# Splitting the first layers of a fused attention + gated FFN kernel into two rounds over the batch pairs

## The chip, the cores and the metric

One core of one Trainium2 chip runs the whole kernel. The metric is the device time of one execution in microseconds (us); lower is better. Engine names below: PE is TensorE, DVE is VectorE, ACT is ScalarE, POOL is GpSimd, SP is SyncE, whose queue issues every DMA of this kernel.

## The reference

Sigmoid attention over 8 batches, 12 heads, 448 positions, head size 64, and behind it a gated feed-forward layer (3584 tokens, model size 768, hidden size 1536).

```python
scores = scale * np.matmul(q, k.transpose(0, 1, 3, 2)) - np.log(S)
attn = 1.0 / (1.0 + np.exp(-scores))
x = (attn @ v).transpose(0, 2, 1, 3).reshape(B * S, H * D)
gate = 1.0 / (1.0 + np.exp(-(x @ w_gate)))
val = x @ w_val
return (gate * val @ w_out).astype(np.float32)
```

The three weight matrices arrive as 64-bit floats; the kernel reads them as 32-bit words and turns them into 16-bit operands itself.

## The kernel before

**Attention.** A beat is one step (m, g): m runs over 24 groups of four heads of a batch, g over 7 key tiles, 168 beats in all. In a beat PE computes scores (L434, 8 matmuls of 64x64), ACT the sigmoid (L437), and PE multiplies an earlier beat's result with v (L451, 8 matmuls). Twice per m, `finish` copies one accumulator out of PSUM on ACT (L461), DVE adds the other (L468), and the sum is stored in DRAM (L473, tensors `xd`).

**Weight conversion.** A group is one 128-column-pair slice (jp, t) of the gate (t = 0) or value (t = 1) matrix, or one k of the output matrix: 12 first-layer groups for 6 d_ff tile pairs jp, and 6 output groups. A group has four chunks of 128 x 384 words. The generator `convert` runs in steps. Two steps per chunk decode the words: DVE L188, L190, L199, L200, L201, L202 and POOL L189. One further step later the chunk's largest absolute value, or its sum of absolutes, is taken (L117 on DVE beside the attention, L114 on ACT later). When the group's scale is known (for first-layer groups over a round trip through DRAM: `rowm` out, `all` back in), seven steps each make one operand: some with a POOL sum (L244), all with a 16-bit cast `whl` on POOL (L342, beside the attention) or ACT (L339, later), and in the next step the remainder on DVE (L214); one step after that the pair is sent to DRAM (L222, tensors `ad` and `oo`). `due` and `BESIDE` say how many steps are run in each tick or beat. Nine groups (`FIRST`) are converted beside the attention, three in the first visit, six output groups later.

**First layers (A visits).** The batches are handled as four pairs, by a seven-product scheme on 2 x 2 blocks (`N_OPS` = 7). A visit ("A", pr) runs 6 jp x 2 (gate, value) x 7 = 84 products; a product is 9 matmuls (L569) of 16-bit high and low parts. A product is one tick. `unit` adds the seven products up on DVE, POOL and ACT (L554, L582, L584), then come sigmoid (L730), scaling (L339), and the product of gate and value (L745 on DVE, L747 on POOL). Products fill one of 8 PSUM buffers. `load_operands` keeps a ring of 8 weight operands, up to 11 ahead with those that stay resident: 24 of the 84 stay in the `held` tiles of the hidden values (`RESIDENT`). Beside a visit the next pair's x is read from `xd` and subtracted (`load_x`, L309 on POOL, from tick 8 on every second tick) and split into the pairs of 16-bit operands `b` (`split_x`, L339 on ACT, L345 on DVE, from tick 56, `SPLIT`). Hidden values go to DRAM, those of the last pair stay (`hold`).

**Output layer (C visits).** Pairs in reversed order, 21 products of 18 matmuls each. `Operands` makes 16-bit operands `hh`, `hl` (L339, L345) from the hidden values; `OutScale` finds a scale per pair from all hidden values, over the same kind of round trip through DRAM (`rowh`, `all`). Products 0 to 5 use a scale from half of the hidden values, the later ones the whole.

The order on each engine is the order in which the program emits instructions, and an engine that waits holds up all that stands behind it:

```python
visits = [("A", pr) for pr in pairs] + [("C", pr) for pr in reversed(pairs)]
```

Of the kernel before, what the change touches and what calls it, by code (L numbers as in the profile page):

```python
# [33 lines left out]
FIRST = 9  # L34
# [10 lines left out]
SPLIT = 56  # L45
# [3 lines left out]
def sigmoid_attention_glu_kernel(ctx: ExitStack, tc: tile.TileContext, qk, v, wg, wv, wo, out):  # L49
# [154 lines left out]
    def convert(words, parts, ks, largest_of, cast):  # L204
# [5 lines left out]
        def split():  # L210

            while unsplit:
                x, sc, hl, where = unsplit.pop(0)
                nc.vector.scalar_tensor_tensor(out=hl[:, 1], in0=x, scalar=sc.s, in1=hl[:, 0], op0=ALU.mult, op1=ALU.subtract)  # L214
                unsent.append((hl, where))
# [9 lines left out]
        def high(x, sc, where):  # L225
            hl = pool.tile([P, 2, CW], F16, tag="whl", name="whl", bufs=words.held)
            cast(hl[:, 0], x, sc.s)
            unsplit.append((x, sc, hl, where))
# [65 lines left out]
    def convert_steps(n_groups, everywhere):  # L294
        return 8 * n_groups + (TAIL + 2 if everywhere else TAIL - 3)
# [10 lines left out]
    visits = [("A", pr) for pr in pairs] + [("C", pr) for pr in reversed(pairs)]  # L306
# [44 lines left out]

    def split_x(pr, cast=scaled):
# [3 lines left out]
        for at in range(len(work) + 2):  # L356
            if at >= 2:
                hi, lo = new_bs[work[at - 2]]
                n, k = work[at - 2]
                rest(lo, source(n, k), x_scales[pr].s, hi)  # L360
                if n == 2:
                    subtract(nc.gpsimd, xs[5, k], xs[2, k], xs[5, k])
            if 1 <= at <= len(work):
                n, k = work[at - 1]
                at_, half = divmod(at - 1, 2)
                if not half:
                    both = operand_pairs(at_)
# [5 lines left out]
    N_A = 2 * JPS * N_OPS  # L373
    RESIDENT = range(12, 84, 3)

    def visit_operands(v_):
        kind, _ = visits[v_]
        if kind == "A":
            return [(a_dram[jp][t][n].rearrange("p a f -> p (a f)"), [("a", jp, t, n)],
                     r if r in RESIDENT and v_ < len(pairs) - 1 else None)  # L380
                    for r, (jp, t, n) in enumerate(itertools.product(range(JPS), range(2), range(N_OPS)))]
# [4 lines left out]
    ring, resident, new_resident = [], {}, [None]  # L386

    def load_operands(most=RING + BEYOND):

        while wanted and len(ring) < most:  # L390
            source, keys, r = wanted[0]
            if r in resident:
                ring.append((resident[r], False))
            else:
                if r is None and sum(own for _, own in ring) == RING:
                    break
                a = new_resident[0]() if r is not None else xpool.tile([P, 2 * KC * P], F16, tag="A", name="A", bufs=RING)
                assert all(key in stored for key in keys), keys
                nc.sync.dma_start(out=a, in_=source)
                if r is not None:  # L400
                    resident[r] = a
# [8 lines left out]
    with tc.manual_schedule(), tc.tile_pool(name="att", bufs=2) as att, tc.tile_pool(name="sc", bufs=2, space=PSUM) as scp, \  # L410
# [47 lines left out]
        def finish(n):  # L458
# [3 lines left out]
            adds.append((x, avs.pop((n, 1))[:, :S]))  # L462
            stores.append((beat + 2, b, c, x))

        def finish_adds():
            while adds:
                x, other = adds.pop()
# [28 lines left out]
        words = Words(att, chunks(halves_of_jps[:FIRST], ()), AHEAD, 4)  # L496
        weights, n_weights, done = convert(words, halves_of_jps[:FIRST], (), max_abs, scaled_gpsimd), convert_steps(FIRST, True), 0
# [11 lines left out]
        for m in range(B * NQ):  # L509
            for g in range(7):  # L510
# [8 lines left out]
                beat += 1  # L519
                while done < n_weights and done * BESIDE < beat * n_weights:  # L520
                    next(weights)
                    done += 1
                finish_adds()
# [9 lines left out]
        beat += 2  # L533
# [101 lines left out]
    def hold(pr):  # L635
        big = {}
        for i in range(4):
            for k in range(KH):
# [3 lines left out]
                hs[pr, i, k] = big[at][:, k % 2 * S:k % 2 * S + S]  # L642

# [44 lines left out]
    def a_visit(v_):  # L688

        pr, nxt = visits[v_][1], visits[v_ + 1]  # L690
        bs.update(new_bs)
        keep = nxt == ("C", pr)
        following = next((p for kind, p in visits[v_ + 1:] if kind == "A"), None)
        x_loads = load_x(following, new_raw) if following is not None else iter(())
        splits = split_x(following) if nxt[0] == "A" else iter(())
        if keep:
            hold(pr)
            chain[0] = Operands([p for _, p in itertools.takewhile(lambda x: x[0] == "C", visits[v_ + 1:])])
# [3 lines left out]
        def tick():  # L702
# [5 lines left out]
            if p >= N_A - 22 and p % 2 == 0 and early:  # L708
# [8 lines left out]
            if p >= N_A - 6:  # L717
# [215 lines left out]
```

## Time and profile before

| | |
|---|---|
| median of 3 runs | 1271.9 us (1268.73 to 1272.67) |
| profiled execution | 1265.04 us, span 1263.3 us |
| busy, share of the span | PE 92%, DVE 70%, POOL 50%, ACT 48% |
| DMA | 244.61 MB, 68.6% of 16 engines' time |
| mean granted TensorE clock | 0.966 |

Busy time is summed for each engine, and engines overlap, so the shares do not add up. What a change in one stage is worth is read from that stage's own stretch of the span: how long it took beside the time that its matmuls need when nothing holds them. A wait is put down to the instruction that released it. The 64x64 score matmuls and the 128x128 ones have different durations, so a stretch is compared only with a stretch of the same kind.

### The profile page before, as it was taken

The page shows a single profiled execution, that of the slowest core. Times are in us where ns is not written, and L with a number is a line of the kernel's source. Part 1 is how long each engine was busy: PE and PEld are TensorE (multiplying, and loading weights), DVE is VectorE, ACT ScalarE, POOL GpSimd, SP SyncE. Part 2 cuts the span into 40 slices and gives each one's busy share as a digit, 9 for nine tenths or more (in the row PEclk, how much of TensorE's full clock was granted, in tenths as well). Part 3 has the DMA queues.
Part 4 walks back from the last instruction along what each step waited for, and adds up shares of the span by engine and source line. Part 5 has one row for each costly group of instructions (what it writes and reads, how often), then busy time and mean ns, then how long its engine had stood idle before and what let it go on. Part 6 is the DMA issues. An engine that isn't in the chain of part 4 may idle for free.

```text
span 1263.3 us, 20978 instructions
## 1 busy us (share of the span) xinstructions
PE 1161.1 (92%) x7240; PEld 564.3 (45%) x7240; DVE 889.5 (70%) x1502; ACT 610.5 (48%) x1111; POOL 632.9 (50%) x544
## 2 busy tenths in 40 slices
PE   9988777879999959999999998999994989999998
PEld 3433333334455424555445553455552445555554
DVE  5677777775378958569887897684354858676773
ACT  6754544546554356543565545544442424344240
POOL 0354656688335535356444654353255629293660
PEclk9998888889999989999999999999997999999999
DMA  8889878857699765766458864565543787776734
GB/s 295 216 229 250 243 224 234 201 169 230 198 286 201 196 137 180 230 170 178 129 184 258 188 188 117 158 162 145 139 121 78 131 269 219 241 237 209 244 114 149
DMA packets 176554, 244.61 MB, mean 194 GB/s; under 512 B 52160, under 2 KB 160960, under 8 KB 176448
## 3 DMA queue, kind: packets, MB, share of 16 engines
q1 hardware_dynamic: 176448, 243.28, 68.6%
q8 instruction: 56, 0.92, 0.3%
q14 instruction: 50, 0.41, 0.1%
HBM read 179.90 MB, written 63.32 MB: 193 GB/s over the span
## 4 chain that ended last, share of the span: by engine, by line
PE 55%; DVE 15%; DMA 10%; POOL 9%; issue 7%; ACT 3%; SPq 0%; DVEq 0%; POOLq 0%; ACTq 0%
PE un L569 49%; POOL whl L342 3%; PE sc L434 3%; PE av L451 3%; DVE whl L214 2%; POOL wf L244 2%; DVE wf L200 2%; DVE wf L199 1%; DVE wm L201 1%; DVE hl L345 1%; DMA rowh<-h02m 1%; DMA xd<-x 1%; DMA all<-rowh 1%; POOL wf L189 1%; POOL v L309 1%
## 5 line engine op out<-in xcount | busy, mean ns | idle before, releaser
L569 PEld LDWEIGHTS <-A 128*128 128x128 f16 x3888 | 382.5, 98 | 416.1 <-issue 56.7
L569 PE MATMUL un<-b,A 128*128 128x448 f16 x2376 | 469.4, 356 | 26.8 <-DVE u L554 15.1
L569 PE MATMUL un<-hh,A 128*128 128x448 f16 x1008 | 275.5, 355 | 6.5 <-ACT hh L339 3.5
L451 PE MATMUL av<-a,v 64*64 64x448 f32 x1344 | 244.2, 570 | 39.5 <-DVE x L468 35.8
L434 PE MATMUL sc<-qk 64*64 64x448 f32 x1344 | 241.8, 574 | 4.1 <-DMA qk<-qk 4.0
L437 ACT ACTIVATE a<-sc,bias 128x896 f32<-128x896 f32 x168 | 169.3, 1008 | 140.4 <-PE sc L434 122.1
L569 PE MATMUL un<-hl,A 128*128 128x448 f16 x504 | 179.2, 356 | 16.7 <-DVE hl L345 16.7
L554 POOL TENSOR_TENSOR u<-u,p 128x448 f32<-128x448 f32 x48 | 59.5, 1240 | 193.7 <-DVE u L554 165.1
L569 PE MATMUL un<-b,v 128*128 128x448 f16 x648 | 135.4, 354 | 3.2 <-ACT p L582 2.1
L451 PEld LDWEIGHTS av<-a,v 64*64 64x64 f32 x1344 | 83.0, 141 | 118.3 <-issue 56.8
L434 PEld LDWEIGHTS sc<-qk 64*64 64x64 f32 x1344 | 82.0, 142 | 93.2 <-issue 80.7
L189 POOL TENSOR_SCALAR wf<-wf 128x384 f32<-128x384 f32 x72 | 39.5, 549 | 165.7 <-DVE wf L188 165.7
L730 ACT ACTIVATE g<-c,back 128x448 f32<-128x448 f32 x96 | 62.0, 659 | 79.6 <-DVE c L554 74.0
L569 PEld LDWEIGHTS <-v 128*128 128x128 f16 x648 | 63.8, 98 | 64.6 <-issue 6.7
L309 POOL TENSOR_TENSOR b<-b 128x448 f32<-128x448 f32 x48 | 67.1, 1433 | 47.0 <-DVE hl L345 47.0
L309 POOL TENSOR_TENSOR v<-v 128x448 f32<-128x448 f32 x48 | 66.8, 1423 | 40.4 <-DVE hl L345 26.5
L244 POOL TENSOR_TENSOR wf<-wf 128x384 f32<-128x384 f32 x72 | 75.9, 1058 | 13.7 <-DVE whl L214 13.5
L114 ACT ACTIVATE junk<-g 128x448 bf16<-128x448 f32 x72 | 41.4, 575 | 84.0 <-DVE g L745 68.6
L554 DVE TENSOR_TENSOR c<-un,u 128x448 f32<-128x448 f32 x96 | 58.3, 616 | 21.5 <-PE un L569 19.9
L554 DVE TENSOR_TENSOR u<-un,p 128x448 f32<-128x448 f32 x48 | 29.8, 621 | 60.7 <-PE un L569 49.1
L554 POOL TENSOR_TENSOR c<-u,p 128x448 f32<-128x448 f32 x48 | 59.6, 1242 | 25.1 <-DVE u L554 24.6
L200 DVE SCALAR_TENSOR_TENSOR wf<-wraw,wf 128x384 uint32<-128x384 uint32 x72 | 58.3, 809 | 2.5
(336 smaller groups left out, 1466.3 us busy)
## 6 DMA issues: line engine op xcount, KB each, us to landing
A<-ad SPq DMA_DIRECT2D x264, 192.0 KB, 3.1
A<-oo SPq DMA_DIRECT2D x168, 192.0 KB, 2.9
qk<-qk SPq DMA_DIRECT2D x23, 896.0 KB, 7.3
ad<-whl SPq DMA_DIRECT2D x84, 192.0 KB, 4.4
h<-g SPq DMA_DIRECT2D x72, 224.0 KB, 2.7
v<-vv SPq DMA_DIRECT2D x24, 448.0 KB, 6.7
xd<-x SPq DMA_DIRECT2D x48, 224.0 KB, 6.0
b<-h SPq DMA_DIRECT2D x48, 224.0 KB, 3.6
```

The costliest lines, as they stand in the source:

```text
L114: nc.scalar.activation(junk[:, :x.shape[-1]], x, AF.Abs, accum_out=to)
L189: nc.gpsimd.tensor_scalar(out=f, in0=f, scalar1=F32_MAX, scalar2=F64_ZERO, op0=ALU.min, op1=ALU.max)
L200: nc.vector.scalar_tensor_tensor(out=e, in0=raw[:, :, 1], scalar=0xC0000000, in1=e, op0=ALU.bitwise_and, op1=ALU.bitwise_or)
L244: nc.gpsimd.tensor_tensor(out=x, in0=y, in1=z, op=op)
L309: engine.tensor_tensor(out=to, in0=x, in1=y, op=ALU.subtract)
L342: nc.gpsimd.tensor_scalar(out=to, in0=x, scalar1=s, scalar2=None, op0=ALU.mult)
L434: nc.tensor.matmul(sc[halves[u], h, :S], lhsT=qkt[halves[h], p, k0:k0 + HP], rhs=qkt[halves[h], p, :S], start=True, stop=True)
L437: nc.scalar.activation(a, sc[:, :, :S], AF.Sigmoid, bias=bias, scale=scale)
L451: nc.tensor.matmul(avs[key][halves[h], :S], lhsT=vt[halves[u], g, h], rhs=a[halves[u], h], start=start, stop=g == last)
L554: engine.tensor_tensor(out=to, in0=x, in1=y, op=ALU.add)
L569: nc.tensor.matmul(acc, lhsT=w, rhs=m, start=i == 0, stop=i == len(terms) - 1)
L730: nc.scalar.activation(gates[i], acc, AF.Sigmoid, scale=units[0])
```

## The change

The first layers are run in two parts. Part 0 covers jp 0 to 3 (d_ff tiles 0 to 7), 56 products, pairs 0, 1, 2, 3. Part 1 covers jp 4 and 5 (tiles 8 to 11), 28 products, pairs 3, 2, 1, 0. The output layer then runs pairs 0, 1, 2, 3.

```diff
-FIRST = 9
+FIRST = 7
-SPLIT = 56
+JPS_OF_PARTS = (range(0, 4), range(4, 6))
-    visits = [("A", pr) for pr in pairs] + [("C", pr) for pr in reversed(pairs)]
+    visits = [("A", pr, 0) for pr in pairs] + [("A", pr, 1) for pr in reversed(pairs)] + [("C", pr, None) for pr in pairs]
+    n_a = 2 * len(pairs)
```

Pairs 0, 1 and 2 need their x operands twice. After the split they are stored in DRAM (11 DMAs a pair, 4.8 MB), also in the split of pair 0 beside the attention, and read back one visit ahead:

```diff
+    def load_b(pr):
+        for at in range(KEPT + 1):
+            both = operand_pairs(at)
+            nc.sync.dma_start(out=both, in_=b_dram[pr, at])
...
+            while unsent:
+                nc.sync.dma_start(**unsent.pop(0))
...
+                if pr != pairs[-1] and (half or at_ == KEPT):
+                    b_dram[pr, at_] = dram.tile([P, 2 * half + 2, S], F16, name=f"bd{pr}_{at_}")
+                    unsent.append(dict(out=b_dram[pr, at_], in_=stores_of[at_]))
```

Seven weight groups are converted beside the attention; the eighth in ticks 2 to 30 of the first visit; the other ten in 190 ticks of visits 1 to 6, which is where `calm` says. The remainder on DVE (L214) comes two steps after the cast beside the attention, not one (`lag`), the order of the operands is changed, `whl` has 6 buffers there, not 4. The additions of the attention's two accumulators (L468) are emitted at the start of the next beat, their stores one beat later than before.

```diff
-    def convert(words, parts, ks, largest_of, cast):
+    def convert(words, parts, ks, largest_of, cast, lag, drain_after):
...
-            while unsplit:
-                x, sc, hl, where = unsplit.pop(0)
+            while unsplit and unsplit[0][0] + lag <= now:
+                _, x, sc, hl, where = unsplit.pop(0)
...
-            for x, n in ((a11, 0), (a12, 4), (a22, 6)):
+            for x, n in ((a22, 6), (a11, 0), (a12, 4)):
...
-            if at == len(parts):
+            if at == drain_after:
                 yield from drain()
...
-            stores.append((beat + 2, b, c, x))
+            stores.append((beat + 3, b, c, x))
...
+        words = Words(att, chunks(halves_of_jps[:FIRST], ()), AHEAD, 6)
+        weights = convert(words, halves_of_jps[:FIRST], (), max_abs, scaled_gpsimd, 2, None)
...
+    weights = convert(words, halves_of_jps[FIRST:], range(KH), sum_abs, scaled, 1, 1)
...
+    n_one = convert_steps(1, True, 1)
+    n_all = 8 * (2 * JPS - FIRST - 1) + convert_steps(KH, False, 1)
+    calm = [t for v_ in range(1, n_a - 1) for t in range(starts[v_] + 2, starts[v_] + 31 if v_ < 3 else starts[v_ + 1])]
...
+    for ticks, n in ((range(2, 31), n_one), (calm, n_all)):
```

Resident weight operands are chosen per part: 24 of 56 and 24 of 28, so that 216 loads from `ad` are left of 288. In a part-0 visit the next pair's x is read in ticks 2 to 13 and subtracted to tick 30; its split begins at tick 31. The last A visit (pair 0, part 1) keeps its own 8 hidden tiles of 24 and reads the other 16 back in its first 16 ticks:

```diff
+    def resident(part, r):
+        return r >= RING and r % 2 == 1 if part == 0 else r % N_OPS > 0
...
+        return (nc.sync.dma_start(out=hs[pr, i, k], in_=h_dram[pr, i, k]) for i in range(4) for k in range(KH) if (i, k) not in kept)
...
+        if nxt[2] == 0:
+            x_loads, splits = load_x(nxt[1], new_raw), split_x(nxt[1])
+        elif not keep and nxt[1] != pr:
+            moves = load_b(nxt[1])
...
-            if p >= 8 and p % 2 == 0:
+            if 2 <= p < 14 or p >= 14 and p % 2 == 0:
                 next(x_loads, None)
-            if p >= SPLIT:
+            if p >= 31:
                 next(splits, None)
+            next(moves, None)
```

More of the change, by code (lines that the diff above doesn't have):

```diff
@@ L227, in high @@
             cast(hl[:, 0], x, sc.s)
-            unsplit.append((x, sc, hl, where))
+            unsplit.append((now, x, sc, hl, where))
         def to_a(jp, t, n):
@@ L355, in split_x @@
         source = lambda n, k: xs[(0, 4, 5, 1, 2, 3, 5)[n], k]
-        for at in range(len(work) + 2):
+        unsent = []
+        for at in range(len(work) + 3):
+            while unsent:
+                nc.sync.dma_start(**unsent.pop(0))
+            if at == len(work) + 2:
+                yield
+                break
             if at >= 2:
@@ L461, in finish, with finish_adds @@
             nc.scalar.copy(x, avs.pop((n, 0))[:, :S])
-            adds.append((x, avs.pop((n, 1))[:, :S]))
-            stores.append((beat + 2, b, c, x))
-        def finish_adds():
-            while adds:
-                x, other = adds.pop()
+            adds.append((beat, x, avs.pop((n, 1))[:, :S]))
+            stores.append((beat + 3, b, c, x))
+        def finish_adds(wait=0):
+            while adds and adds[0][0] + wait < beat + (not wait):
+                _, x, other = adds.pop(0)
                 nc.vector.tensor_tensor(out=x, in0=other, in1=x, op=ALU.add)
@@ L532, in sigmoid_attention_glu_kernel @@
             finish_adds()
-        beat += 2
+        beat += 3
         finish_stores()
@@ L633, in finish, with hold @@
                 outs.setdefault((self.pr, n), self)
-    def hold(pr):
+    def hold(pr, jps):
+        kept = {(2 * (jp // KC) + t, 2 * (jp % KC) + j) for jp in jps for t in range(2) for j in range(2)}
         big = {}
@@ L688, in a_visit @@
     def a_visit(v_):
-        pr, nxt = visits[v_][1], visits[v_ + 1]
+        (_, pr, part), nxt = visits[v_], visits[v_ + 1]
+        jps = JPS_OF_PARTS[part]
+        n_p = 2 * len(jps) * N_OPS
         bs.update(new_bs)
[L692 to L695, printed above, removed]
+        keep = nxt[0] == "C"
+        x_loads = splits = moves = iter(())
+        if nxt[2] == 0:
+            x_loads, splits = load_x(nxt[1], new_raw), split_x(nxt[1])
+        elif not keep and nxt[1] != pr:
+            moves = load_b(nxt[1])
         if keep:
-            hold(pr)
-            chain[0] = Operands([p for _, p in itertools.takewhile(lambda x: x[0] == "C", visits[v_ + 1:])])
+            moves = hold(pr, jps)
+            chain[0] = Operands([p2 for kind, p2, _ in visits if kind == "C"])
         p, unsent, unsummed = 0, [], []
@@ L858, in sigmoid_attention_glu_kernel, with make_resident @@
     shared = {}
-    def make_resident():
-        i, half = divmod(len(resident), 2)
+    def make_resident(part):
+        i, half = divmod(sum(key[0] == part for key in residents), 2)
         if not half:
@@ L882, in beside, with before_last @@
     def beside(v_, p):
-        if v_ <= last_conv:
-            for _ in range(due.get(N_A * v_ + p, 0)):
-                next(weights)
-    def before_last(v_):
-        if v_ == last_conv:
-            assert next(weights, None) is None and not list(weights)
-            stage.close()
-            stage.enter_context(tc.manual_schedule())
-            oper[0] = stage.enter_context(tc.tile_pool(name="oper", bufs=1, reuse_waits="tile"))
-    for v_, (kind, _) in enumerate(visits):
+        for _ in range(due.get(starts[v_] + p, 0)):
+            next(weights)
+    def before_last():
+        assert next(weights, None) is None and not list(weights)
+        stage.close()
+        stage.enter_context(tc.manual_schedule())
+        oper[0] = stage.enter_context(tc.tile_pool(name="oper", bufs=1, reuse_waits="tile"))
+    for v_, (kind, *_) in enumerate(visits):
         (a_visit if kind == "A" else c_visit)(v_)
```

64 lines of the change are left out of this document (29 added, 35 removed).

## The prediction

> **What bounds the kernel now.** I first read the page's head, then cut the span at the stages (by the count of matmuls: 756 for an A visit, 378 for a C visit) and asked for each stretch's busy times, and last for the waits in those that are longer than their matmuls need.
>
> ```profile
> span 1263.3 us, 20978 instructions
> PE 1161.1 (92%) x7240; PEld 564.3 (45%) x7240; DVE 889.5 (70%) x1502; ACT 610.5 (48%) x1111; POOL 632.9 (50%) x544
> ```
>
> ```profile
> 0.00:62.00 62.00, 60.55 (x616) 24.16 (x620) 36.32 (x88) 43.68 (x49) 11.89 (x20) 1.00 0.87 259
> 62.00:290.00 228.00, 185.90 (x1671) 74.83 (x1660) 174.03 (x350) 117.10 (x135) 143.85 (x130) 0.90 0.81 218
> 290.00:332.70 42.70, 41.27 (x427) 19.05 (x426) 19.02 (x32) 29.50 (x35) 29.23 (x23) 1.00 0.68 235
> 332.70:498.50 165.80, 148.84 (x759) 74.98 (x758) 126.77 (x220) 83.57 (x191) 75.96 (x68) 0.96 0.76 202
> 498.50:646.70 148.20, 144.06 (x758) 73.91 (x756) 113.54 (x194) 76.33 (x179) 70.59 (x63) 1.00 0.61 176
> 646.70:802.90 156.20, 147.29 (x758) 74.77 (x757) 128.56 (x218) 85.02 (x198) 78.69 (x71) 0.98 0.65 183
> 802.90:946.00 143.10, 143.10 (x758) 74.03 (x757) 79.17 (x138) 64.84 (x139) 58.91 (x52) 1.00 0.55 146
> 946.00:1044.80 98.80, 75.54 (x380) 37.78 (x378) 62.88 (x104) 31.41 (x57) 47.78 (x36) 0.90 0.64 161
> 1044.80:1116.30 71.50, 71.50 (x380) 36.98 (x379) 52.14 (x58) 28.41 (x48) 41.79 (x31) 1.00 0.76 232
> ...
> 25.00:50.00 25.00, 25.00 (x272) 10.25 (x268) 15.60 (x40) 18.66 (x22) 2.35 (x5) 1.00 0.84 229
> ```
>
> The columns are the stretch, its length, busy time and instruction count of PE, its weight loads, DVE, ACT and POOL, the granted clock, the share of the DMA engines and GB/s. The undisturbed rows give the floors: the fourth A visit, 84 products in 143.10 us, so 1.703 us a product; a C visit 71.5; in the attention 272 matmuls in 25 us. The 1671 matmuls of 62 to 290 would then take 153.6 us; the stretch takes 228, so 74 us are lost there, the largest loss. The A visits lose 22.7, 5.1, 13.1 and 0, the first C visit 27.3. All other stretches are at their floor.
>
> ```profile
> DVE whl L214 <- POOL whl L342: 50.5, 30, 2.7
> ...
> PE av L451 <- DVE x L468: 35.0, 14, 4.8
> ...
> SPq L473 <- DVE x L468: 48.3, 17, 7.5
> ```
>
> These are the waits of DVE, PE and SP's queue in 62 to 290: who waited for whom, us in total, times, the longest. DVE is busy for 174.0 and waits 50.5 for POOL's cast: 224.5 of 228. PE waits for DVE's addition, which stands behind the conversion. So DVE, with that wait, bounds the attention from the time the operands are made.
>
> **The change, part by part.**
>
> *Two weight groups leave the attention.* Rows over the whole attention, 36 chunks each:
>
> ```profile
> L202 DVE SCALAR_TENSOR_TENSOR wf<-wm,wf 128x384 f32<-128x384 uint32 x36 | 24.6, 684 | 1.2
> L200 DVE SCALAR_TENSOR_TENSOR wf<-wraw,wf 128x384 uint32<-128x384 uint32 x36 | 24.3, 674 | 1.2
> L201 DVE SCALAR_TENSOR_TENSOR wm<-wraw,wm 128x384 uint32<-128x384 uint32 x36 | 19.7, 548 | 0.0
> L199 DVE TENSOR_SCALAR wf<-wf 128x384 uint32<-128x384 uint32 x36 | 16.4, 455 | 1.6 <-POOL wf L189 1.6
> L188 DVE TENSOR_SCALAR wf<-wraw 128x384 uint32<-128x384 uint32 x36 | 13.1, 363 | 7.9 <-DMA wraw<-wg 7.9
> L190 DVE TENSOR_SCALAR wm<-wraw 128x384 uint32<-128x384 uint32 x36 | 12.7, 353 | 0.0
> L117 DVE TENSOR_REDUCE w01c<-wf 128x1 f32<-128x384 f32 x4 | 2.2, 551 | 0.1
> ...
> 62.00:290.00 228.00, 47.82 (x51) 0.90 0.81 218
> ```
>
> The six decoding rows sum to 110.8, over nine groups 12.3 each; the reduction is 2.2; the last row is L214 alone, 0.94 us each, seven to a group 6.6. A group costs DVE 21.1 us, two 42.2; 51 of the 63 L214 lie in the stretch, so I take 51/63 of it, 34 us, out of 174: 140 remain. That is under PE's 153.6, so PE becomes the bound there.
>
> *The remainder two steps after its cast.* 73 steps (8 x 7 + 17) in 160 beats are 2.2 beats, over 3 us, apart, and the cast with the POOL sum ahead of it is a little over 2 us. Before, a late DVE met the cast at once. Of the 50.5 us of waiting I keep 10; the bounds are 0 and 7/9 of it, 39. Additions one beat later change no order on DVE, and the stores no longer hold SP (48.3 us of its waiting).
>
> *Sum for the attention.* DVE 150, PE 153.6, coupled by few buffers: the nearest row in which both are heavily used is the first A visit, PE 148.84 of 165.8, 90%. 153.6 / 0.90 = 171, a gain of 57. Bounds: PE's floor gives 74; DVE 140 + 39 at 90% gives 199, a gain of 29. The b stores of pair 0 (4.8 MB) replace nearly what two groups moved (8 chunks of 393 KB, 14 operands of 197 KB, 5.9 MB), so the DMA load stays.
>
> *A visits.* Durations of DVE from the second and third visit (498.5 to 802.9):
>
> ```profile
> L554 DVE TENSOR_TENSOR c<-un,u 128x448 f32<-128x448 f32 x48 | 29.1, 615 | 7.6 <-PE un L569 6.0 <-ACT g L730 1.5
> L745 DVE SCALAR_TENSOR_TENSOR g<-c,back,g 128x448 f32<-128x448 f32 x24 | 26.7, 1112 | 0.8
> L200 DVE SCALAR_TENSOR_TENSOR wf<-wraw,wf 128x384 uint32<-128x384 uint32 x21 | 20.8, 990 | 0.7
> L345 DVE SCALAR_TENSOR_TENSOR b<-r,x2s,b 128x448 f16<-128x448 f32 x21 | 18.0, 858 | 7.1 <-ACT b L339 7.0
> L201 DVE SCALAR_TENSOR_TENSOR wm<-wraw,wm 128x384 uint32<-128x384 uint32 x21 | 17.1, 815 | 0.0
> L199 DVE TENSOR_SCALAR wf<-wf 128x384 uint32<-128x384 uint32 x21 | 15.1, 719 | 0.0
> L202 DVE SCALAR_TENSOR_TENSOR wf<-wm,wf 128x384 f32<-128x384 uint32 x21 | 13.3, 635 | 0.7
> L190 DVE TENSOR_SCALAR wm<-wraw 128x384 uint32<-128x384 uint32 x22 | 10.6, 480 | 0.0
> L188 DVE TENSOR_SCALAR wf<-wraw 128x384 uint32<-128x384 uint32 x22 | 10.5, 477 | 0.0
> L214 DVE SCALAR_TENSOR_TENSOR whl<-wf,o2s,whl 128x384 f16<-128x384 f32 x7 | 7.2, 1022 | 0.2 <-ACT whl L339 0.2
> ...
> L214 DVE SCALAR_TENSOR_TENSOR whl<-wf,o0s,whl 128x384 f16<-128x384 f32 x7 | 4.7, 669 | 0.0
> ```
>
> A chunk is 4.12 us, four 16.5; seven remainders at 0.85 (between the two L214 rows) 5.9; about 1 for the scale: 23.4 us a group. The sums of 56 products cost 40 x 0.615 + 8 x 1.11 + small ones 2.4 = 36 us, those of 28 products 18. A split is 18.
>
> Visit 0: 36 + 18 + 23.4 = 77 of 95.4 us (56 x 1.703), one group where three were, and the eighth group is stored by tick 31 while its first load is due at tick 38 or later: 3 lost instead of 22.7. Visit 1 (14 steps, mostly decoding, 29): 83 of 95.4: 0, and up to 10 if the x subtractions on POOL stretch DVE there. Visit 2: 14 steps at 7 chunks and 12 remainders, 42: 96 of 95.4, and in its first 31 ticks 61 against 52.8; the 8 PSUM buffers (13.6 us) cover most: 5.
>
> Visits 3 to 6 hold the rest of ten groups, 234 - 29 - 42 = 163, and 36 + 54: 253 against 140 x 1.703 = 238. DVE is over by 15, and I take 15. Bounds: with POOL never in the way 0 (next fence); twice the excess, 30, since the first visit before lost 22.7 where a burst of two groups' operands and the split exceeded its ticks by about half as much.
>
> Visit 4 also reads 28 operands, b of the next pair, weight words and stores operands and hidden values, about 16.6 MB in 47.7 us, 348 GB/s. The nearest rate without a PE wait:
>
> ```profile
> 350.00:375.00 25.00, 25.00 (x134) 12.92 (x132) 19.28 (x35) 14.83 (x40) 9.23 (x10) 1.00 0.92 299
> ```
>
> At 299 GB/s it takes 8 us more; the 11 operands ahead cover part: 4, bounds 0 and 8. In all, 33 stores and 33 loads of b, 16 stores and 16 loads of hidden values come to SP and 72 operand loads go: 26 more issues, off the path; behind a b store that waits for DVE stand operand loads with 8 products of slack.
>
> *First C visit.* Its loss stays, 27: the scale of the whole pair still needs the last values, and the round trip is not shortened:
>
> ```profile
> PE un L569 <- DVE hl L345: 16.7, 1, 16.7
> ```
>
> *Sum.* Feed-forward losses before 22.7 + 5.1 + 13.1 + 27.3 = 68; after 3 + 0 + 5 + 15 + 4 + 27 = 54: gain 14, bounds -12 (10 + 10 + 30 + 8 + 27, less 5 for not all at once) and 41 (27 alone). With 57: gain 71. The profiled execution took 1265.0 us, so 1194; the median of the runs is 6.9 above it, so **1201**.
>
> **Where the Trainium skill is weighed.** DVE without POOL (first two rows) and beside it:
>
> ```profile
> 430.03 0.35 DVE L199 TENSOR_SCALAR wf<-wf 128x384 uint32<-128x384 uint32 x1
> 430.42 0.56 DVE L200 SCALAR_TENSOR_TENSOR wf<-wraw,wf 128x384 uint32<-128x384 uint32 x1
> 432.71 1.37 POOL L554 TENSOR_TENSOR u<-u,p 128x448 f32<-128x448 f32 x1 [3.02 <-DVE u L554]
> 433.01 1.29 DVE L188 TENSOR_SCALAR wf<-wraw 128x384 uint32<-128x384 uint32 x1
> ```
>
> L188 takes 1.29 us where its like takes 0.35, and ends as POOL's sum does. So DVE time is not a fixed cost; alone, a group is about 16 us (three operations a chunk at 0.35, three at 0.56, a remainder taken at 0.56 too), 110 for the late visits' share, and with 81 for the sums they need 191 of 238: hence the bound of 0 above. The Trainium skill, "SBUF — State Buffer", section "Who interferes with whom", calls the port pair of the two engines an exclusive lock: whoever starts first holds it for the whole instruction. The trace agrees here (1.29 against 0.35). By that rule DVE's work alone on SBUF operands (110, and 14 for L745) and POOL's (0.89 us a product as in the second and third visit, (70.59 + 78.69) / 168, so 124) add up to 248 in visits 3 to 6, an excess of 10 in place of 15, and the sum would be 5 us lower.
>
> **The rivals.**
> - *DMA bounds the attention.* 228 us at 218 GB/s are 49.7 MB, unchanged. At 259, the rate of the first 62 us with a share of 0.87, they take 192 us: gain 36, so 1222. For: shares of 0.81 to 0.87 already. Against: 299 GB/s was reached beside a full PE. Chance 0.20.
> - *Visits 2 to 6 fall behind by twice the excess*, for POOL's sums and DVE's remainders hold each other up: 15 becomes 30, 5 becomes 10, and 8 for the transfers: 24 more, 1225; with DVE at 90% useful as well, 1235. Chance 0.18.
> - *Slower.* The conversion in visits 3 to 6 sets their pace. It decides only if a group costs DVE 34 us there, not 23.4 (163 becomes 234, and the 71 are gone); no row has such a price. 1280. Chance 0.06.
> - *No gain in the attention*: DVE's addition stays late, since it stands behind whole steps as before; only the 14 remain, 1258. Against: DVE's 34 us of work are gone whatever the order. Chance 0.04.
>
> **How the numbers follow.** My forecast has 0.52. The median of this kernel can be told from no change at about 0.3%, 4 us: only the slower case, and a sliver of the fourth, lie there or above. Faster 0.91, same 0.03, slower 0.06. The likeliest case's own range is 1178 to 1220 (attention gain 40 to 74, feed-forward 54 give or take 12); the two middle rivals take the range up to 1238, below it I go to 1172 for an attention at PE's floor with little lost in the late visits.
>
> **What would show it.** Attention: matmuls end near 275 us (332.7 before), L214 hardly waits for L342, PE above 85% busy in the middle. Visit 0 with gaps under 3 us in sum. Visits 3 to 6: DVE busy over 95% and PE waiting for DVE at L554; if PE never waits, POOL was less in the way than I take. First C visit: one gap of about 17 us before a matmul on `hl`. Wrong if PE in the attention waits for qk or v, or if the late visits lose over 30 us.

## The result and the profile after

Measured: **1205.9 us** (median of 4 runs, 1204.3 to 1208.4) against 1271.4 us for the kernel before (median of 4 runs, 1268.7 to 1272.7); ratio **0.9489**, 95% interval 0.9465 to 0.9513. The forecast was 1201. The profiled execution took 1204.3 us.

The head of the page of the changed kernel:

```profile
span 1202.5 us, 21029 instructions
PE 1138.0 (95%) x7240; PEld 566.3 (47%) x7240; DVE 889.1 (74%) x1494; ACT 621.8 (52%) x1141; POOL 626.0 (52%) x530
```

DVE's and POOL's busy time is what it was (889.5 and 632.9): the work has not shrunk, it has been put elsewhere. The same kind of stretches as in the prediction (length; busy time and count of PE, PE's weight loads, DVE, ACT, POOL; granted clock; DMA share; GB/s). The attention ends at 278.1; then come visits 0 to 2, visit 3, visits 4 to 6 together, visit 7, the first C visit and the other three:

```profile
0.00:62.00 62.00, 60.60 (x616) 24.20 (x620) 32.17 (x78) 43.55 (x49) 8.82 (x16) 1.00 0.85 258
62.00:240.00 178.00, 167.24 (x1693) 78.34 (x1686) 147.88 (x287) 118.68 (x137) 129.95 (x111) 0.97 0.93 267
240.00:278.00 38.00, 38.00 (x408) 18.11 (x400) 15.16 (x21) 28.05 (x32) 20.56 (x16) 1.00 0.79 273
278.00:376.00 98.00, 95.72 (x508) 49.24 (x505) 65.50 (x113) 54.84 (x124) 47.53 (x40) 1.00 0.84 246
376.00:471.40 95.40, 95.40 (x506) 49.36 (x505) 82.17 (x129) 55.78 (x132) 52.91 (x45) 1.00 0.76 228
471.40:570.90 99.50, 95.79 (x505) 49.18 (x504) 85.50 (x144) 59.45 (x139) 54.20 (x47) 1.00 0.70 179
570.90:676.90 106.00, 99.80 (x506) 50.28 (x505) 93.97 (x182) 51.51 (x120) 51.90 (x50) 0.97 0.65 183
676.90:834.60 157.70, 148.28 (x758) 74.45 (x756) 132.35 (x238) 78.30 (x181) 78.95 (x75) 0.98 0.80 254
834.60:882.30 47.70, 47.70 (x254) 24.69 (x253) 22.00 (x40) 21.18 (x43) 17.30 (x15) 1.00 0.76 206
882.30:984.10 101.80, 74.78 (x379) 37.58 (x378) 63.07 (x104) 31.42 (x57) 47.73 (x36) 0.88 0.64 156
984.10:1202.50 218.40, 214.72 (x1136) 110.86 (x1133) 149.34 (x164) 79.05 (x134) 116.13 (x84) 1.00 0.65 201
```

Lengths less floors (1.703 us a product in the A visits, 71.5 us for a C visit) give this account; the last column is the prediction's.

| stretch | before | after | forecast |
|---|---|---|---|
| attention, length | 332.7 | 278.1 | 276 |
| A visits, lost | 40.9 | 32.1 | 27 |
| of it visits 0, 1, 2 | | 2.6, 0, 4.2 | 3, 0, 5 |
| of it visits 3 to 6 | | 10.6, 4.1, 6.2, 4.4: 25.3 | 15 + 4 |
| first C visit, lost | 27.3 | 30.3 | 27 |

So 55 us come from the attention and 9 from the A visits, and 3 go back in the first C visit: 61, which is the difference of the two spans (1263.3 and 1202.5).

The waits over the attention, 0 to 278: one row of DVE's, then PE's. Lines have moved in the changed kernel: POOL's cast is L343 (L342 before), the addition L490 (L468), the attention's matmuls L456 and L473 (L434, L451), a product's matmul L592 (L569), its sum L577 (L554).

```profile
DVE whl L214 <- POOL whl L343: 3.1, 4, 1.1
...
PE sc L456 <- DMA qk<-qk: 6.6, 4, 3.5
PE av L473 <- DMA v<-vv: 3.8, 3, 2.4
...
PE av L473 <- DVE x L490: 0.2, 1, 0.2
```

DVE's 50.5 us of waiting for the cast have become 3.1, and PE no longer waits for DVE's addition (35.0 before, 0.2 now). What PE waits for now are transfers, and PE's busy share of the middle (62 to 240) is 94%. A busy PE is not always at full speed there: its matmuls of the middle take 167.2 us, and at the rate of the undisturbed row (272 in 25 us) the 1693 would take 155.6. So of the 22 us over that floor about 11 are gaps and 12 are slower matmuls, at a mean granted clock of 0.97. In the middle before, the same split gives 42 us of gaps and 32 of slower matmuls (185.9 for 153.6) at a clock of 0.90; the prediction's 74 us did not tell the two apart.

### The profile page after: what moved, and what is told of

The parts are those of the page before. It is cut to its first block, busy times and chain, and to the rows that moved or that the text cites. A ratio compares the mean times of both kernels' runs of the same rounds, so it can differ in the third digit from the quotient of the medians.

```text
span 1202.5 us, 21029 instructions
## 1 busy us (share of the span) xinstructions
PE 1138.0 (95%) x7240; PEld 566.3 (47%) x7240; DVE 889.1 (74%) x1494; ACT 621.8 (52%) x1141; POOL 626.0 (52%) x530
## 4 chain that ended last, share of the span: by engine, by line
PE 59%; DMA 15%; DVE 14%; issue 5%; POOL 4%; ACT 3%; SPq 0%; DVEq 0%; POOLq 0%; ACTq 0%
PE un L592 42%; PE sc L456 8%; PE av L473 8%; DMA qk<-qk 4%; DVE whl L214 2%; DMA A<-oo 2%; DVE wf L200 1%; DVE wf L199 1%; DVE c L577 1%; POOL wf L244 1%; DMA A<-ad 1%; DVE hl L346 1%; DVE wm L201 1%; DVE wf L188 1%; DMA u<-xd 1%
## 5 line engine op out<-in xcount | busy, mean ns | idle before, releaser
L592 PEld LDWEIGHTS <-A 128*128 128x128 f16 x3024 | 297.0, 98 | 317.0 <-issue 33.3
L592 PE MATMUL un<-b,v 128*128 128x448 f16 x1512 | 309.0, 356 | 14.1 <-DVE c L577 6.9
L592 PE MATMUL un<-b,A 128*128 128x448 f16 x1512 | 306.5, 355 | 7.5 <-ACT p L605 4.1
L592 PE MATMUL un<-hh,A 128*128 128x448 f16 x1008 | 275.1, 355 | 9.8 <-DMA A<-oo 9.8
L592 PEld LDWEIGHTS <-v 128*128 128x128 f16 x1512 | 148.6, 99 | 158.4 <-issue 19.6
L592 PE MATMUL un<-hl,A 128*128 128x448 f16 x504 | 178.8, 355 | 17.2 <-DVE hl L346 17.2
L456 PE MATMUL sc<-qk 64*64 64x448 f32 x1344 | 183.9, 547 | 6.6 <-DMA qk<-qk 6.6
L473 PE MATMUL av<-a,v 64*64 64x448 f32 x1344 | 184.3, 545 | 4.1 <-DMA v<-vv 3.8
L577 POOL TENSOR_TENSOR u<-u,p 128x448 f32<-128x448 f32 x48 | 59.5, 1240 | 185.2 <-DVE u L577 144.8
L189 POOL TENSOR_SCALAR wf<-wf 128x384 f32<-128x384 f32 x72 | 40.2, 558 | 170.4 <-DVE wf L188 165.2
L456 PEld LDWEIGHTS sc<-qk 64*64 64x64 f32 x1344 | 65.2, 136 | 81.3 <-issue 62.1
L473 PEld LDWEIGHTS av<-a,v 64*64 64x64 f32 x1344 | 65.5, 135 | 73.0 <-issue 59.9
L310 POOL TENSOR_TENSOR v<-v 128x448 f32<-128x448 f32 x48 | 66.8, 1423 | 40.9 <-DVE hl L346 26.5
L577 POOL TENSOR_TENSOR c<-u,p 128x448 f32<-128x448 f32 x48 | 62.9, 1311 | 17.0 <-DVE u L577 17.0
L490 DVE TENSOR_TENSOR x<-av,x 128x448 f32<-128x448 f32 x48 | 29.7, 619 | 52.4 <-ACT x L483 52.4
L777 POOL TENSOR_TENSOR g<-c,g 128x448 f32<-128x448 f32 x44 | 58.2, 1336 | 14.4 <-DVE c L577 13.9
L577 DVE TENSOR_TENSOR c<-un,u 128x448 f32<-128x448 f32 x96 | 57.5, 614 | 8.3 <-PE un L592 6.8
```

The lines of the kernel that those rows point to most:

```text
L189: nc.gpsimd.tensor_scalar(out=f, in0=f, scalar1=F32_MAX, scalar2=F64_ZERO, op0=ALU.min, op1=ALU.max)
L310: engine.tensor_tensor(out=to, in0=x, in1=y, op=ALU.subtract)
L456: nc.tensor.matmul(sc[halves[u], h, :S], lhsT=qkt[halves[h], p, k0:k0 + HP], rhs=qkt[halves[h], p, :S], start=True, stop=True)
L473: nc.tensor.matmul(avs[key][halves[h], :S], lhsT=vt[halves[u], g, h], rhs=a[halves[u], h], start=start, stop=g == last)
L490: nc.vector.tensor_tensor(out=x, in0=other, in1=x, op=ALU.add)
L577: engine.tensor_tensor(out=to, in0=x, in1=y, op=ALU.add)
```

## The experiments

The later runs were made on other chips, where the kernel before took 1260 to 1264 us. So ratios are compared, and stretches of the traces. In six profiles (the changed kernel's among them) in which the attention was the same it took 273 to 281 us, and in eight in which the first C visit was the same it lost 24 to 30: smaller differences than that are not told apart by one profile. The 30.3 of the changed kernel is the highest of those eight.

### What the attention's gain is made of

**before_lag2**: the kernel before with the later remainder alone.

```diff
-            while unsplit:
-                x, sc, hl, where = unsplit.pop(0)
+            while unsplit and unsplit[0][0] + lag <= now:
+                _, x, sc, hl, where = unsplit.pop(0)
...
-        words = Words(att, chunks(halves_of_jps[:FIRST], ()), AHEAD, 4)
-        weights, n_weights, done = convert(words, halves_of_jps[:FIRST], (), max_abs, scaled_gpsimd), convert_steps(FIRST, True), 0
+        words = Words(att, chunks(halves_of_jps[:FIRST], ()), AHEAD, 6)
+        weights, n_weights, done = convert(words, halves_of_jps[:FIRST], (), max_abs, scaled_gpsimd, 2), convert_steps(FIRST, True) + 1, 0
```

> The kernel before with nine groups beside the attention, and only the remainder two steps after its cast (and 6 buffers for the pairs in place of 4). Theory (DVE's work of 174 us in the stretch 62 to 290 and its wait of 50.5 us add up to the bound): the wait falls to about 10, DVE at 184 of work and wait becomes the bound at some 90 to 95%, the stretch takes 195 to 205 us, and the total is 1243 to 1253, ratio 0.978 to 0.986. Rival (the work alone bounds, the wait only fills time that DVE would lose elsewhere): ratio 0.995 to 1.0.

The operands' order is the old one here, so one remainder in a group is taken from a value that a sum has already replaced; the instructions are the same in number and kind. Ratio 0.9791 (0.9766 to 0.9816). Its attention ends at 304.3 us; the stretch from 62 that holds the same work, and two of DVE's waits in it:

```profile
62.00:262.00 200.00, 169.98 (x1651) 73.19 (x1644) 173.96 (x343) 115.44 (x133) 149.87 (x129) 0.97 0.90 247
...
DVE whl L214 <- POOL wf L244: 6.2, 6, 1.4
...
DVE whl L214 <- POOL whl L342: 1.4, 2, 1.1
```

DVE's work is the same 174 us, and the stretch went from 228 to about 202 (1671 matmuls where the row has 1651) with nothing taken away but the wait. The wait had two sides: within a step POOL's clamp of the decoded words (L189) waits for DVE's L188, POOL's cast stands behind it, and DVE's next step begins with the remainder of that cast. In the middle before, DVE waited 50.5 us for POOL and POOL 55.3 for that row of DVE's; here POOL waits 18.6. The theory holds: the attention is 28 us shorter by the step between cast and remainder alone. The two buffers added for the pairs are not what does it: the next run keeps six and has the wait back.

**lag1**: the changed kernel with that step undone.

```diff
-        weights = convert(words, halves_of_jps[:FIRST], (), max_abs, scaled_gpsimd, 2, None)
+        weights = convert(words, halves_of_jps[:FIRST], (), max_abs, scaled_gpsimd, 1, None)
...
```

> The changed kernel with one edit undone: beside the attention the remainder (L214) again comes one step after its cast instead of two. Theory (the wait for the cast was half of DVE's excess, and the second step takes it away): DVE's wait of L214 for L343 grows from 3 us to 30 to 40 us, the attention from 278 us to 290 to 303, and the total is 12 to 25 us longer, ratio to the kernel before 0.958 to 0.968. Rival (the two groups fewer are enough, PE is the bound by a margin): the wait grows as much, but the attention stays within 4 us of 278 and the ratio stays at 0.947 to 0.952.

Ratio 0.9562 (0.9515 to 0.9610). The attention's waits and its middle:

```profile
DVE whl L214 <- POOL whl L343: 37.3, 26, 2.7
...
PE av L473 <- DVE x L490: 12.9, 7, 3.3
...
62.00:250.00 188.00, 169.09 (x1690) 75.91 (x1682) 143.57 (x284) 118.35 (x136) 122.17 (x108) 0.96 0.88 252
```

The wait is back as forecast (37 us) and PE waits for the addition again. The attention ended at 288.7, 11 us later, just under the theory's 290 to 303 and above the rival's 282: with seven groups the step is worth about 11 (8 to 15, by the spread of the attention between profiles), with nine 28. The two parts overlap: with the step first they are worth 28 and 26, with the groups first 44 and 11. The numbers for the groups hold the other edits to the attention too; adds_old and no_b, below, find no worth in two of these that can be measured.

**first8**: one group back into the attention.

```diff
-FIRST = 7
+FIRST = 8
```

> The changed kernel with eight groups beside the attention instead of seven, so one group fewer in the visits. Theory (with seven groups DVE has just come under PE's floor in the attention, and the late visits are set by DVE's conversion work): 17 us more on DVE in the attention's middle bring it level with PE, the attention takes 284 to 292 us; visits 1 to 6 (the first has no conversion left but the drain) lose 8 to 14 us less; total within 6 us of the changed kernel, ratio 0.944 to 0.953. Rival (the attention is by now held by transfers, not by DVE): attention 276 to 281, ratio 0.937 to 0.943.

Ratio 0.9455 (0.9435 to 0.9476). The middle of the attention, and visits 0 to 2 and 3 to 6:

```profile
62.00:248.00 186.00, 168.82 (x1692) 79.57 (x1688) 162.14 (x317) 118.54 (x137) 138.58 (x120) 0.99 0.97 269
...
286.10:576.00 289.90, 287.84 (x1516) 148.43 (x1513) 229.35 (x382) 170.15 (x392) 154.42 (x130) 0.99 0.73 217
576.00:823.80 247.80, 240.46 (x1261) 122.94 (x1260) 213.02 (x386) 123.68 (x285) 125.25 (x119) 1.00 0.76 231
```

The attention takes 286.1 us, 8 more, for 14 more of DVE's work (162.1 for 147.9); the visits lose 13.2 in place of 32.1 (3.9 in visit 2, 9.3 in visits 3 to 6). So DVE, no longer the bound at seven, is level with PE at eight, and in the profiles one group fewer takes 19 us from the visits' loss, one more costs the attention 8. By the intervals the total cannot be told from that of seven. The first visit still converts one group, now the ninth, whose row w40m is written at 316.4 us; the expectation was wrong to leave it nothing but the drain.

**adds_old**: additions and stores placed as before.

```diff
-            stores.append((beat + 3, b, c, x))
+            stores.append((beat + 2, b, c, x))
...
-                finish_adds(1)
                 while done < n_weights and done * BESIDE < beat * n_weights:
                     next(weights)
                     done += 1
+                finish_adds()
```

> The changed kernel with the attention's additions emitted at the end of their own beat and their stores one beat earlier, as before. Theory (the order on DVE is the same either way, only SP is freed): SP's wait for L490's line grows from 24 us to 35 to 50, PE's time stays within 4 us of 278 and the ratio at 0.947 to 0.953. Rival (late additions held PE's accumulators, 35 us of PE's waiting before): PE waits for the additions by over 8 us again and the ratio is 0.956 or more.

Ratio 0.9497 (0.9469 to 0.9525), attention 278.7 us, PE's wait for the addition 2.6. SP's wait for it was 28.7 us, short of the forecast 35. No part of the gain that can be measured comes from their placing.

### What the late visits lose

**half_out**: three of the six output groups, pace unchanged, so none in visits 5 and 6.

```diff
-    words = Words(conv, chunks(halves_of_jps[FIRST:], range(KH)), AHEAD_FF, 4)
+    words = Words(conv, chunks(halves_of_jps[FIRST:], range(KH // 2)), AHEAD_FF, 4)
...
-    weights = convert(words, halves_of_jps[FIRST:], range(KH), sum_abs, scaled, 1, 1)
+    weights = convert(words, halves_of_jps[FIRST:], range(KH // 2), sum_abs, scaled, 1, 1)
...
```

> The changed kernel with only three of six output groups converted (each is stored twice, so that stores stay nearly the same); the pace of the steps stays, so the conversion ends in visit 4 and visits 5 and 6 have none. What is left out: three groups' decoding, sums, casts and remainders. Theory (the late losses come from the conversion on DVE): visits 5 and 6 lose under 1.5 us together instead of 10.6, visits 2 to 4 lose what they lost (15 to 22 us in sum), ratio 0.937 to 0.943. Rival (the b reads and the stores at a visit's start hold PE): visits 5 and 6 still lose 6 us or more, ratio 0.945 or above.

Ratio 0.9415 (0.9392 to 0.9437). Visit 4, then visits 5 and 6:

```profile
676.90:731.10 54.20, 49.05 (x254) 24.03 (x252) 35.91 (x65) 26.04 (x59) 23.63 (x22) 1.00 0.96 289
731.10:826.50 95.40, 95.40 (x506) 49.33 (x505) 37.83 (x64) 36.41 (x80) 33.04 (x29) 1.00 0.57 194
```

Visits 5 and 6 are at their floor (56 x 1.703 = 95.4), though they still read b for the next pair. Visit 3 still loses 9.0, visit 4 6.5. So there is no loss in visits 5 and 6 without the conversion, and the reads alone cause none.

**no_b**: no stores and reads of the x operands.

```diff
-                if pr != pairs[-1] and (half or at_ == KEPT):
+                if False and (half or at_ == KEPT):
...
-            moves = load_b(nxt[1])
+            pass
```

> The changed kernel without the stores and the reads of the x operands in DRAM: visits 5 to 7 use pair 3's operands. What is left out: the right operands of three visits, and 29 MB of transfers. Theory (transfers are hidden but for a few us): attention shorter by 0 to 4 us, visits 4 to 6 lose 0 to 5 us less of 15, the total 0 to 8 us less, ratio 0.942 to 0.949. Rival (DMA is what holds the attention's rest over its floor, 22 us in 62 to 240, and visits 4 to 6): attention 8 to 15 us shorter and visits 4 to 6 without loss, ratio 0.925 to 0.935.

Ratio 0.9441 (0.9420 to 0.9463). Attention 275.1, inside the spread; visit 4 loses 2.1 in place of 4.1, visits 3, 5 and 6 about what they lost (9.2, 6.2, 4.4). Visits 3 to 6:

```profile
565.50:825.80 260.30, 245.35 (x1261) 124.64 (x1260) 224.17 (x417) 128.01 (x296) 131.15 (x125) 0.98 0.61 173
```

By the ratios the total is 6 us lower, and the 29 MB cost a few us at most: the theory's 0 to 8, not the rival's.

**no_sums**: POOL's sums left out.

```diff
-                nc.gpsimd.tensor_tensor(out=x, in0=y, in1=z, op=op)
-                high(x, sc, to(n))
+                if sums:
+                    nc.gpsimd.tensor_tensor(out=x, in0=y, in1=z, op=op)
+                high(x if sums else y, sc, to(n))
...
-    weights = convert(words, halves_of_jps[FIRST:], range(KH), sum_abs, scaled, 1, 1)
+    weights = convert(words, halves_of_jps[FIRST:], range(KH), sum_abs, scaled, 1, 1, False)
```

> The changed kernel with POOL's sums (L244) left out of the conversion in the visits; casts and remainders take an unsummed operand, so DVE, ACT and DMA do what they did. 20 to 25 us less of POOL beside visits 0 to 6. Theory (POOL's instructions stretch DVE's on SBUF operands, and the cast waits for the sum): DVE's mean durations in the late visits fall (L200 from 0.76 us to 0.65 to 0.72, L214 likewise), its wait for the cast halves, and the late loss of 29 us falls to 15 to 22, ratio 0.938 to 0.945. Rival (DVE's count of instructions sets the loss, POOL does not matter): durations and loss stay, ratio 0.946 to 0.952.

Ratio 0.9285 (0.9260 to 0.9310), more than the theory gave. Visits 3 to 6 and DVE's decoding in them, without the sums; then the same two rows of the changed kernel:

```profile
559.80:803.40 243.60, 239.36 (x1262) 123.05 (x1261) 215.23 (x419) 128.27 (x299) 93.55 (x90) 1.00 0.79 244
...
L200 DVE SCALAR_TENSOR_TENSOR wf<-wraw,wf 128x384 uint32<-128x384 uint32 x27 | 18.3, 678 | 0.9
L199 DVE TENSOR_SCALAR wf<-wf 128x384 uint32<-128x384 uint32 x27 | 14.1, 522 | 0.0
```

```profile
L200 DVE SCALAR_TENSOR_TENSOR wf<-wraw,wf 128x384 uint32<-128x384 uint32 x27 | 20.5, 759 | 0.9
L199 DVE TENSOR_SCALAR wf<-wf 128x384 uint32<-128x384 uint32 x27 | 18.4, 681 | 0.0
```

All visits together lose 5.4 us in place of 32.1, visits 3 to 6 5.2 in place of 25.3, with DVE executing as many instructions (419 in both). DVE's busy time fell by 11 us and its wait for the cast over visits 2 to 6 from 25.7 to 11.6. The sums left out were 49 us of POOL in all visits (44 of about 1.1 us), 38 of them in visits 3 to 6, twice what the expectation took. So POOL's sums, on an engine busy for half of the time, set most of the late loss, by DVE instructions that take longer, by a late operand, or by both; the run does not separate the two ways. late_lag2, below, takes away the wait alone and wins 7 us. The stretching is uneven: L199, L188, L201 and L200 got shorter by 10.0 us together, but L202 (558 ns) and, against the expectation, L214 (47.7 us for 60 in both) did not change.

The Trainium skill ("SBUF — State Buffer", section "Who interferes with whom") says that VectorE and GpSimd contend for a shared port pair, as an exclusive lock. The rows that got shorter fit that rule; L202 and L214, unchanged, show no effect of it here.

**late_lag2**: the remainder two steps later in the visits too.

```diff
-    weights = convert(words, halves_of_jps[FIRST:], range(KH), sum_abs, scaled, 1, 1)
+    weights = convert(words, halves_of_jps[FIRST:], range(KH), sum_abs, scaled, 2, 1)
...
```

> The changed kernel with the remainder two steps after its cast in the visits too (one buffer more for the pairs, one fewer for a sum, to fit). In visits 2 to 6 the changed kernel loses 29 us (4.2, 10.6, 4.1, 6.2, 4.4), and DVE waits there 24 us for ACT's cast. Theory (in the late visits DVE's work and its waits are the bound, as they were in the attention): the wait falls under 8 us and the loss to 12 to 20 us, ratio to the kernel before 0.936 to 0.943. Rival (the excess is work and the POOL port, or the transfers; the wait is slack): the wait falls and the loss stays within 4 us, ratio 0.946 to 0.952.

Ratio 0.9436 (0.9412 to 0.9460). DVE's largest wait in visits 2 to 6, of the changed kernel, and below it with the later remainder:

```profile
DVE whl L214 <- ACT whl L340: 25.7, 24, 2.9
```

```profile
DVE u L577 <- ACT p L605: 12.4, 9, 3.0
```

DVE's wait for the cast went from 25.7 us to under 0.5, and visits 2 to 6 lose 22.7 in place of 29.5, so 7 us for 25 of waiting: between the two expectations. In visits 3 to 6 DVE's busy time rose from 226 to 233 us, and the 12.4 us are now waited for ACT's copies out of PSUM. The wait was partly slack.

### The first C visit, and versions that go further

**all4**: four buffers for the fetched rows.

```diff
-            self.all = const.tile([P, P], F32, name="all", tag="all", bufs=2)
+            self.all = const.tile([P, P], F32, name="all", tag="all", bufs=4)
```

> The changed kernel with four buffers instead of two for the tile into which a scale's row is fetched (all). In the first C visit three fetches are issued together, and the third stands in SP's queue until the first buffer is read by DVE, which stands behind work that waits for operand loads behind that fetch. Theory: the second group of gaps (7.9 + 2.6 us at products 25 and 29, PE waiting for A from oo) goes to under 3 us, the visit loses 17 to 22 us instead of 24 to 30, ratio to the kernel before 0.940 to 0.945. Rival (SP is held by the round trip of the row itself, buffers or not): the gaps stay and the ratio is 0.947 to 0.952.

PE's waits in the first C visit, of the changed kernel, and below it with four buffers:

```profile
PE un L592 <- DVE hl L346: 17.2, 1, 17.2
PE un L592 <- DMA A<-oo: 9.8, 2, 7.5
```

```profile
PE un L592 <- DVE hl L346: 16.2, 1, 16.2
PE un L592 <- DMA A<-oo: 2.4, 1, 2.4
```

The second wait is nearly gone and the visit loses 21.2 us. The ratio, 0.9447 (0.9401 to 0.9492), is too wide to tell.

**c_other**: pair 1 first.

```diff
-... + [("C", pr, None) for pr in pairs]
+... + [("C", pr, None) for pr in C_ORDER]     # [1, 0, 2, 3]
...
-            moves = hold(pr, jps)
+            moves = hold(nxt[1], ())
...
-        early = OutScale(pr, 1).steps() if keep else []
+        early = [lambda fs=fs: [f() for f in fs] for fs in zip(*(OutScale(p2, 2).steps() for p2 in C_ORDER if p2 != pr))] if keep else []
...
```

> The changed kernel with the output layer begun by pair 1 (order 1, 0, 2, 3), whose hidden values are all in DRAM by visit 6: the last A visit reads its 24 hidden values and makes the scales of pairs 1, 2 and 3 in its first 14 ticks, pair 0's own values go to DRAM like the others' and its scale is made within the first C visit; four buffers for the fetched rows. Theory (the first C visit loses its time to the round trip of the scale that needs the last A visit's values, and to the rows of the others): its loss falls from 24 to 30 us to under 5, ratio 0.926 to 0.933. Rival (POOL's and DVE's backlog of the operands' subtractions at the change of stages holds PE anyway): the loss stays above 12 us, ratio 0.936 or above.

Ratio 0.9348 (0.9302 to 0.9393), between the two expectations. The last A visit, and the first C visit:

```profile
838.10:890.60 52.50, 47.81 (x253) 24.38 (x252) 25.19 (x60) 20.85 (x43) 16.63 (x15) 1.00 0.87 241
```

```profile
890.60:966.70 76.10, 73.58 (x380) 37.42 (x379) 60.25 (x75) 31.27 (x57) 49.15 (x36) 0.98 0.75 219
```

The first C visit loses 4.6 us: the theory holds there. But the last A visit, at its floor of 47.7 without this edit, loses about 5, PE waiting 4.7 for operand loads.

**best**: the edits of first8, late_lag2 and c_other together.

> Eight groups beside the attention, the remainder two steps after its cast everywhere, and the output layer begun by pair 1 with the scales made early. Theory (the three act in different stretches and add up: 4, 6 and 22 us of about 1200): attention 283 to 289 us, visits 0 to 6 lose 8 to 14 us, the first C visit under 5, ratio 0.916 to 0.926. Rival (eight groups and the later remainder take the same loss away twice, or the late visits then meet the transfers): ratio 0.927 to 0.935.

1171.5 us on a chip where the kernel before took 1263.5; ratio **0.9274** (0.9233 to 0.9315), just inside the rival's range, with an interval that reaches into the theory's. Attention 286.0, visits 0 to 6 lose 10.9, the first C visit 4.0, as forecast; but the last A visit loses 8.9, which is about what is missing.

**best_act**: for that visit.

```diff
-            nc.sync.dma_start(out=self.row.rearrange("o p -> p o"), in_=self.m)
+            (nc.scalar if self.name[0] == "h" else nc.sync).dma_start(out=self.row.rearrange("o p -> p o"), in_=self.m)
...
-        def steps(self):
-            return [self.rows, self.send, idle, self.fetch, idle, idle, self.finish]
+        def steps(self, trip=1):
+            return [self.rows, self.send] + [idle] * trip + [self.fetch, idle, idle, self.finish]
...
```

> The version with eight groups, the later remainder and pair 1 first, and two edits more for the last A visit, which lost 8.9 us there: the rows of the output scales (rowh) are written by a DMA from ACT's queue, not SP's, and the rows are fetched six ticks later. Theory (operand loads on SP's queue waited 7.4 and 4.4 us behind the slow write of a row): the last A visit loses under 3 us, ratio to the kernel before 0.918 to 0.925. Rival (the 28 operand loads and 24 loads of hidden values in that visit are too much for the transfers): it still loses 5 us or more, ratio 0.926 to 0.932.

Ratio 0.9297 (0.9280 to 0.9315): no better. The visit loses 4.4, between the two expectations, and the ratio lies in the rival's range: the queue was half of the 8.9 at most. The trace shows what else is there: 4 us windows of this run; the three rows are sent from 824.26 on:

```profile
824.26 0.35 ACTq L146 DMA_DIRECT2D rowh<-h12m  x1
...
824.00:828.00 4.00, 4.00 (x23) 2.08 (x22) 1.36 (x5) 0.53 (x1) 1.13 (x1) 1.00 1.34 213
828.00:832.00 4.00, 4.00 (x23) 2.08 (x22) 1.54 (x3) 1.93 (x4) 1.13 (x1) 1.00 0.81 40
832.00:836.00 4.00, 4.00 (x23) 2.08 (x22) 0.62 (x1) 2.40 (x4) 0.00 (x0) 1.00 0.80 49
836.00:840.00 4.00, 1.79 (x10) 0.70 (x8) 0.62 (x1) 0.53 (x1) 1.13 (x1) 1.00 0.68 37
840.00:844.00 4.00, 3.62 (x13) 1.55 (x14) 0.62 (x1) 0.00 (x0) 0.40 (x1) 0.70 0.92 333
```

For 12 us all transfers together move 37 to 49 GB/s, while the DMA engines count as 68 to 81% busy, and PE runs dry at the end of it. That the rows' writes do this is read from the timing; a run that writes them in another form was not made.

## Why the prediction was right

**The total.** Close, in part by luck. From profile to profile the forecast gain was 71 us and the measured one 61: the attention is 2 us longer than forecast, the A visits 5 and the first C visit 3. The forecast of the median, 1201, lies only 5 us from the measured 1205.9, because it adds the 6.9 us by which the profiled execution before was faster than its median; after the change that difference is 1.6.

**The bound in the attention.** Right: DVE's 174 us of work and 50.5 of waiting. before_lag2 takes the wait away by itself, and lag1 brings it back. The work that leaves was put at 34 us of DVE time in the middle, leaving 140; the row says 147.9. Over the whole attention two groups were priced at 42 us, and DVE's busy time fell by 34 (229.4 to 195.2), for rows that stay got longer: L202 from 684 to 770 ns, the remainders of x (L345, now L346) from 0.73 to 0.98 us. The wait was put at 10 and measured 3.1.

**The coupling factor.** The number came out by luck (178 us, and 171 was forecast for a slightly shorter stretch); the reason did not. I divided PE's floor by 0.90 because DVE and PE would hold each other up. In the trace DVE is idle for 30 of the middle's 178 us, 10 of them waiting for ACT's copy, and PE waits for DVE for 0.2 us. The prediction named a sign of being wrong, PE waiting for qk or v, and it came: 10.4 us of such waits, which are nearly all of the gaps. The attention after, cut into 4 us windows, and the issue of one DMA in the first:

```profile
92.00:96.00 4.00, 4.00 (x46) 2.43 (x42) 3.96 (x11) 2.85 (x4) 0.83 (x2) 1.00 1.01 398
96.00:100.00 4.00, 4.00 (x48) 3.01 (x44) 3.93 (x7) 2.93 (x5) 3.80 (x4) 1.00 1.58 155
100.00:104.00 4.00, 4.00 (x42) 2.21 (x33) 0.38 (x1) 2.64 (x3) 0.96 (x1) 1.00 0.59 57
104.00:108.00 4.00, 1.55 (x6) 0.29 (x4) 2.32 (x6) 1.44 (x2) 0.35 (x1) 0.77 0.87 290
...
92.73 0.32 SPq L146 DMA_DIRECT2D roww<-w10m  x1
```

A group's row is written at 92.73; from 96 to 104 the rate falls from 398 to 57 GB/s, the next v arrives late, and PE is busy 1.55 of the 4 us after, at a granted clock of 0.77. The four longest gaps of the middle (2.4, 3.5, 1.1 and 2.2 us) all end 12 to 16 us after the write of a row, and all wait for qk or v. Two of the loads that they wait for stand in the chain that ended last, with their time from issue to landing:

```profile
129.30 13.19 DMA qk<-qk
...
188.84 13.24 DMA qk<-qk
```

They were issued 0.4 and 2.2 us behind the write of a row, and the median load of qk lands after 6.0 us. No run takes the rows' writes out of the attention, so this is read from the timing. The rival "DMA bounds the attention" had part of the truth (its 192 us against 178 measured), but as gaps in the supply, not as an average rate.

**The A visits.** Visits 0 to 2 within 1 us each. Visits 3 to 6 were mis-sized: 25.3 us against 19. The sum was built wrongly though it came near. DVE's work was priced at 253 us and is 226 in the rows (a chunk 3.7 us, not 4.12; there are no x subtractions on POOL in these visits), so DVE is busy 86% and not over 95%. The stretch of visits 3 to 6, and DVE's largest wait in it:

```profile
570.90:834.60 263.70, 248.07 (x1262) 124.73 (x1260) 226.32 (x419) 129.81 (x300) 130.85 (x125) 0.97 0.74 225
```

```profile
DVE whl L214 <- ACT whl L340: 24.4, 21, 2.9
```

The term left out is that wait for the cast, 26 us over visits 2 to 6, of which late_lag2 finds about 7 to be worth PE's time. no_sums shows that most of the loss hangs on POOL's sums; half_out shows that visits 5 and 6 lose nothing without the conversion. The 4 us for visit 4's transfers measured about 2 (no_b), so the excess put at 15 was about 23; the excess of 10 that the prediction works out for an exclusive lock lies further off.

**The first C visit.** Put at 27, it lost 30.3, at the upper end of the spread of unchanged visits; the gap before a matmul on hl is 17.2 us, as foreseen. The account left out that the other 10 us are a third fetch in SP's queue that waits for a buffer, and that an order of the pairs takes the first gap away.

**Rivals.** The conversion did not set the pace of the late visits at 34 us a group, and the attention's gain did not fail for want of an order: adds_old shows that the placing of the additions is worth nothing measurable. The rival with twice the excess came true in small part: visits 2 to 6 lose 29.5 us where the forecast had 24 and this rival 48.

## What to carry to other kernels

When an in-order engine waits for the result of an instruction that it has itself just made possible, put one more step of other work between the two before moving work away: here that was worth 28 us by itself, and the two groups moved after it 26 (moved first, they were worth 44 and the step 11). Work that is moved under matmuls should be counted on every engine that takes part in it, since the less busy one can set the price of the other: DVE was busy 86% of the late visits and POOL 50%, and leaving out 49 us of POOL gave back 27 us of the visits. And a scale that needs the last values of a stage should not be needed by the first work of the next one; another order of independent items takes its round trip off the path.

## What was not expected of the hardware

A DMA that writes a [128 x 1] column into a row in DRAM, 512 bytes in all, goes with a fall of the rate of all transfers. In the two fences above, on SP's queue and on ACT's, the DMA share stays at 0.59 or more while the rate goes from 398 GB/s over 155 to 57, and from 213 to between 37 and 49 for 12 us. It is no accident of these two: in the trace of the kernel before, which writes 21 rows, the stretch from 3 to 8 us behind a write moved 62 GB/s in the mean over all 21, and the stretch from 6 to 1 us ahead of it 198. That the write is the cause is not shown by a run.

In these traces the granted clock is lower behind a gap of PE, and a busy PE then does less: in the kernel before, PE is busy for 1.02 of the 4 us from 92 to 96, and in the 4 us behind it, busy throughout, it does 32 matmuls at a granted clock of 0.64, where the row of 96 to 100 above has 48 at 1.00. So a wait costs more than its own length.
